# Two attentions on one core: where the local attention's exponentials, the small reciprocals and the reload of old rows stand in the schedule

## The chip, the cores and the metric

The kernel runs on one core of a Trainium2 chip, as one launch. The metric is the device time of an execution in microseconds. Before the change three executions took 1604.45, 1605.76 and 1606.44 us; their median, 1605.76 us, is the time before.

## What is computed

Two attention layers over 2048 positions of width 576, each with 32 heads of 18 columns; their outputs stand side by side in `out` (2048 x 1152, float32).

```
A: qkv = x @ wqkv
   logits[s, w] = q[s] . k[s - 2w] * 18**-0.5     w = 0..7, masked where s - 2w < 0
   o[s] = sum over w of softmax(logits[s])[w] * v[s - 2w]
   out[:, :576] = concat of heads(o) @ wo
B: qkv = x @ wqkv
   o = softmax(q @ k.T * 18**-0.5) @ v            every position against every position
   out[:, 576:] = concat of heads(o) @ wo
```

A is a local attention with a window of eight positions; B is full attention. Products with weights are formed from high and low parts of each operand, so one product is three matmuls.

## The kernel before, in words

**Stages.** Until about 420 us the kernel projects the inputs of A and B to queries, keys and values and stores them in DRAM. Then comes the main loop (L1283), which is the attention of B with everything else woven into it. After it only the last sums are left.

**The main loop.** B's 32 heads are 8 groups of 4 (`g`), its queries 4 blocks of 512 (`b`), its keys 16 tiles of 128 (`kt`): 8 x 4 x 16 = 512 steps, step = 64 g + 16 b + kt. A step computes four score tiles of 128 x 512 (`score`, L262; the matmul is L269), takes the exponential of each on ScalarE (L277) and sums the weighted values of the step before on TensorE (`weigh`, L739; the matmuls are L742). So that the exponentials don't overflow, each query's maximum over its keys is needed before its scores: `maximum` (L224) and `parts_of_maximum` (L239) compute score tiles a second time, some blocks ahead (matmul L158), and VectorE reduces each (L166). A plain step has three of these reductions. When a block's maxima are complete, VectorE folds and transposes them (L176, L183), GpSimd splits them in high and low parts (L101, L102) and `place` (L191, its eight DMAs on L195) puts them into two rows of the block's queries; the block's first score waits for these DMAs.

**Double steps.** A's output projection is 32 sums of 288 columns (`sums_of_a`, L1007). Each is woven into two steps that are issued as one (`together`, L1238): eight scores, eight maxima, the matmuls of the sum (L1256), and on ScalarE the copy of the sum (L1276). `MADE` (L45) has for each of A's eight blocks `j` the four steps in which a sum becomes ready; the double step is the next step and the one after it.

**The agenda.** All other work is planned by hand: `plan(start, pieces)` (L111) puts functions at step numbers, and `due()` (L115) issues those of a step behind the step's own work. An engine executes what it was given in that order, so a piece on VectorE, ScalarE, GpSimd or in SyncE's DMA queue holds up all that was issued behind it on the same engine. After a double step the pieces of its first step are issued, then `weigh`, then those of its second step.

**A's attention** (`local`, L900) for block `j` begins at step `AT[j]` = 10, 67, 123, 178, 233, 288, 343, 398. GpSimd multiplies queries with shifted keys (`match`, from AT + 5), VectorE takes the maximum over the window in three halvings (`most`, L941, AT + 31, 32, 33), GpSimd subtracts it (`lower`, L947, AT + 33), ScalarE takes one exponential of 128 x 512 (`exponents`, L950, AT + 35), VectorE adds over the window in three halvings (`total`, L941, AT + 36, 37, 38) and takes two reciprocals (`inverses`, L957, AT + 38, 39), GpSimd scales (`share`, L960, AT + 39) and weighs the values (`weighted`). All of that from `most` on stands `soon` steps earlier; `soon` (L1022) is 3 for j = 0 and 0 otherwise. The result goes through DRAM (`dao`) and comes back in the layout of the sums by `get` (L984), eight steps ahead of the first of its two sums.

**The end of a block of B** (`finish`, L747): the sums' accumulator `po` is copied out as `o`; its denominators are gathered by a small DMA `den<-o` (L785) one step later, VectorE takes their reciprocals (L786) at 8 steps, they go to DRAM (`drec<-den`, L787, 9 steps) and come back spread over the partitions (`rec<-drec`, L788, 13 steps); GpSimd scales and splits (L789 to L791, from 20 steps) and the result is stored in `do` (L777, 26 steps). In the last group the offsets are 1, 6, 7, 10, 13 to 16 (L784).

**The last group** also computes B's output projection. `fetch_old` (L1047) brings back the rows of the 28 heads before (`old rows`), for each block of queries in four chunks of two DMAs, into room that the keys and queries of group 6 held: those of block 0 are `qs<-do`, those of block 1 `ks<-do`. The weights come as `y<-wob` (`load_wo`, L849). All these DMAs are issued by SyncE, in the order of the agenda, and each waits for the landing of the DMA issued eight before it, because the queue has eight semaphores that are used in turn.

Of the kernel before, what the change touches and what calls it, by code (L numbers as in the profile page):

```python
# [22 lines left out]
NG = H // 4  # L23
# [5 lines left out]
NJ = S // AB  # L29
# [3 lines left out]
STEPS = NB * NT  # L33
# [8 lines left out]

AT = [10, 67] + [13 + 55 * j for j in range(2, S // AB)]

MADE = ((88, 96, 112, 128), (144, 160, 176, 192), (200, 208, 224, 240), (253, 256, 272, 288),  # L45
        (307, 320, 336, 352), (362, 368, 384, 400), (417, 432, 440, 448), (474, 476, 478, 480))


def ap(t, *dims):
# [10 lines left out]
def two_attentions(ctx: ExitStack, tc, xa, wa, woa, xb, wb, wob, out):  # L60
# [50 lines left out]
    def plan(start, pieces):  # L111
        for n, f in pieces:
            agenda[start + n].append(f)
# [267 lines left out]
    with (tc.tile_pool(name="x", bufs=1, side="right") as xp,  # L381
# [103 lines left out]
        if True:  # L485
# [195 lines left out]
            for k in range(2, 14):  # L681
                n = 46 if k == 2 else 36 + 4 * k
# [34 lines left out]
            for c, b in order:  # L717
                n = min(128, 3 * D - 128 * c)
                work_list.append(((b % 2, ws[c][0], xas[b][0], slice(0, n), every),
                                  lambda ps, n=n: ps[:n], lambda ps, c=c, b=b, n=n: leave_a(c, b, n, ps)))  # L720
# [26 lines left out]
    def finish(g, b):  # L747
# [33 lines left out]
                later(2, lambda: stack_new(b))  # L781
                plan(step + 2, full(b))

        times = (1, 8, 9, 13, 20, 21, 22, 26) if g < NG - 1 else (1, 6, 7, 10, 13, 14, 15, 16)  # L784
        for at, f in zip(times, (lambda: load(den, o[DH:128:32]),  # L785
                                 lambda: nc.vector.reciprocal(den, den),  # L786
                                 lambda: load(drec[g, b].rearrange("i (p n) -> (i p) n", n=16), den),  # L787
# [112 lines left out]
    def local(j):  # L900
# [79 lines left out]
        def put(i):  # L980
            load(rows(dao[j, i, 0, 0], (DH * SUB, 128), (1, DH * SUB)),
                 ap(st["parts"][i].bitcast(F32), (1, DH * SUB)))
# [24 lines left out]
        def sums_of_a(h, n, alone=True):  # L1007
# [7 lines left out]
            if not alone:  # L1015
# [3 lines left out]
            behind_scores.append(lambda: nc.vector.tensor_add(y, one, y))  # L1019


        soon = 0 if j else 3  # L1022
        pieces = [(33, lower), (35, exponents), (39, share), (60, upper), (61, rest), (64, lambda: put(0)), (66, lambda: put(1))]

        pieces[:0] = [(at, lambda f=f, n=n: f(n)) for f, ats in ((most, (31, 32, 33)), (total, (36, 37, 38)),
                                                                (inverses, (38, 39))) for n, at in enumerate(ats)]
        for c in range(DH // 2):
            pieces.append((39 + 5 * c // 2, lambda c=c: weighted(c)))
        pieces = [(at - soon, f) for at, f in pieces]
        pieces += [(5 + 5 * c // 2, lambda c=c: match(c)) for c in range(DH // 2)]  # L1030

# [2 lines left out]
        pieces += [(16 + 2 * i, lambda i=i: fetch("v", i)) for i in range(4)]  # L1034
        made = [p - AT[j] for p in MADE[j]]
        for n, ends in enumerate((made[:2], made[2:])):
            pieces.append((ends[0] - 8 if not n else max(ends[0] - 8, made[1] + 1) if j < NJ - 1 else made[0] - 8, lambda n=n: get(n)))
            for h in range(2):
                pieces.append((ends[h], lambda h=h, n=n: finished(h, n)))
                producing.add(AT[j] + ends[h] + 1)  # L1040
            pieces.append((ends[1] + 6, lambda n=n: load(out[p0 + 128 * n : p0 + 128 * n + 128, :D], ys["a", j, n])))
# [50 lines left out]
    sums = {}  # L1092
# [125 lines left out]
    for g in range(1, NG):  # L1218
        if g > EARLY:
            plan(STEPS * (g - 2) + 1, [(n, f) for n, f in enumerate(stack_loads(g))])  # L1220
        if g == NG - 1:
            plan(STEPS * g, [(4, lambda: fetch_old(0)), (10, lambda: fetch_old(1, 0, 2)), (14, lambda: fetch_old(1, 2, 4)),
                             (34, lambda: fetch_old(3)),
                             (38, lambda: fetch_old(2))])
            plan(STEPS * g, [(n, lambda t=t, h=h: partial(t, h)) for n, (t, h) in
                             zip((43, 44, 45, 47, 49, 51), [(t, h) for t in range(3) for h in range(2)])])
            plan(STEPS * g, [(62, lambda: outside.append(lambda: first(3, NB - 1, 0)))])
            for b in range(NB - 1):
                producing.update(STEPS * g + NT * (b + 1) + (23, 15, 7)[b] + n for n in range(8))
        plan(STEPS * (g - 1), [(24, lambda g=g: load_v(g))])  # L1230
# [135 lines left out]
```

## Time and profile before

| | |
|---|---|
| three executions | 1604.45, 1605.76, 1606.44 us |
| the profiled execution | 1607.17 us |
| its span, first to last instruction | 1605.4 us |
| TensorE busy | 1586.9 us |
| VectorE busy | 1363.3 us |
| ScalarE busy | 1214.7 us |
| GpSimd busy | 965.1 us |

The span is one execution on the chip; about 1.8 us of the profiled time lie outside it. The main loop's steps can be found in the trace by the score matmuls on L269: there are 2048 of them, four to a step, so the first of step s is number 4s. Step 449 begins at 1397.4 us, step 464 at 1429.7 us, step 470 at 1442.0 us. A busy engine in the profile is one that has an instruction open; matmuls on different rows of the array overlap, so a busy TensorE isn't one that could do no more.

### The profile page before, as it was taken

Reading aid. Unit: us, or ns where it says so; the run is one execution under the profiler, and the core shown is the slowest. Engines: PE = TensorE matmul, PEld = TensorE weight load, DVE = VectorE, ACT = ScalarE, POOL = GpSimd, SP = SyncE. Lnnn points to the kernel's source line nnn. Section 1 sums busy time; section 2 is a strip of 40 time slices with the busy share of each in tenths; the row PEclk is TensorE's granted clock in tenths of the full one; section 3 lists DMA queues with packets and bytes.
Section 4 is the critical chain, followed back from the end, with each engine's and each line's share of the span. In section 5 each row is a group of like instructions: output and inputs, shape, how many; then the busy total and the mean of one; then the engine's idle time right before and its main releaser. Section 6 shows DMA issues by size and latency. Waiting matters only on the chain.

```text
span 1605.4 us, 34964 instructions
## 1 busy us (share of the span) xinstructions
PE 1586.9 (99%) x13276; PEld 962.1 (60%) x13276; DVE 1363.3 (85%) x2315; ACT 1214.7 (76%) x2438; POOL 965.1 (60%) x798
## 2 busy tenths in 40 slices
PE   9999999999999999999999999999999999998998
PEld 7999888999543445444445445445445445445676
DVE  5199899999999999999999999999999999897622
ACT  6423441221699999999999999999999999996655
POOL 2405742211166995895896896797797799780000
PEclk9999999999999999999999999999999999999999
DMA  8937954532312362255326325422632231153311
GB/s 252 235 127 194 263 167 127 159 101 70 73 41 63 75 144 75 58 120 105 73 75 141 77 86 125 102 81 53 139 102 66 61 97 49 51 178 119 130 61 62
DMA packets 188025, 175.66 MB, mean 109 GB/s; under 512 B 119416, under 2 KB 133240, under 8 KB 186128
## 3 DMA queue, kind: packets, MB, share of 16 engines
q1 hardware_dynamic: 182992, 161.88, 37.2%
q0 software_dynamic: 4032, 10.63, 3.2%
q8 instruction: 104, 1.70, 0.5%
q10 hardware_dynamic: 832, 0.92, 0.2%
q14 instruction: 65, 0.53, 0.1%
HBM read 98.77 MB, written 73.47 MB: 107 GB/s over the span
## 4 chain that ended last, share of the span: by engine, by line
PE 90%; DVE 4%; DMA 2%; ACT 1%; POOL 1%; issue 0%; SPq 0%; POOLq 0%; DVEq 0%
PE po L742 28%; PE bank L269 18%; PE bank L158 17%; PE bank L364 15%; PE bank L301 5%; PE bank L1256 4%; PE bank L1129 4%; DVE mx L166 3%; DMA den<-o 1%; ACT e L277 1%; POOL xlo L412 1%; DMA dqk<-olo 1%; PE bank L516 0%; DMA more<-xa 0%; DVE as L941 0%
## 5 line engine op out<-in xcount | busy, mean ns | idle before, releaser
L166 DVE TENSOR_REDUCE mx<-bank 128x2 f32<-128x512 f32 x2048 | 1278.3, 682 | 129.6 <-PE bank L158 95.9
L277 ACT ACTIVATE e<-bank 128x512 f32<-128x512 f32 x2048 | 1047.1, 607 | 71.9 <-PE bank L269 67.1
L158 PE MATMUL bank<-ks,qs 54*128 54x512 f32 (+1 forms) x2466 | 792.6, 382 | 9.6 <-DVE mx L166 8.1
L158 PEld LDWEIGHTS bank<-ks,qs 54*128 54x128 f32 x2466 | 405.6, 185 | 394.3 <-DVE mx L166 345.3
L269 PE MATMUL bank<-qs,ks 56*128 56x512 f32 x2048 | 598.1, 427 | 0.0
L742 PE MATMUL po<-e,v 128*19 128x512 f32 x4096 | 532.4, 599 | 0.0
L269 PEld LDWEIGHTS bank<-qs,ks 56*128 56x128 f32 x2048 | 310.3, 185 | 31.2 <-ACT e L277 24.6
L923 POOL TENSOR_TENSOR pr<-aq,akv 128x1024 f32<-128x1024 f32 x72 | 158.4, 2201 | 15.8 <-DMA akv<-da 13.0
L966 POOL TENSOR_TENSOR pr<-lg,akv 128x1024 f32<-128x1024 f32 x72 | 158.2, 2197 | 0.6
L742 PEld LDWEIGHTS po<-e,v 128*19 128x19 f32 x4096 | 73.9, 97 | 138.3 <-issue 132.9
L927 POOL TENSOR_TENSOR pr<-pr 128x1024 f32<-128x1024 f32 x64 | 152.5, 2383 | 5.0
L692 ACT ACTIVATE ohi<-bank 128x512 f32<-128x512 f32 (+1 forms) x56 | 30.4, 595 | 150.2 <-issue 115.7
L364 PE MATMUL bank<-xhi,ahi 64*128 64x512 f32 (+1 forms) x448 | 113.7, 388 | 0.0
L364 PE MATMUL bank<-xhi,alo 64*128 64x512 f32 (+1 forms) x448 | 109.7, 388 | 0.0
L364 PE MATMUL bank<-xlo,ahi 64*128 64x512 f32 (+1 forms) x448 | 106.7, 388 | 0.1
L1256 PE MATMUL bank<-wohi,at 64*128 64x288 f32 x480 | 103.4, 305 | 0.0
L967 POOL TENSOR_TENSOR pr<-pr 128x512 f32<-128x512 f32 x72 | 92.5, 1284 | 5.6
L1256 PEld LDWEIGHTS bank<-wohi,at 64*128 64x128 f32 x480 | 74.8, 184 | 27.5 <-ACT e L277 23.8
L412 POOL TENSOR_TENSOR alo<-raw,ahi 128x512 fp32r<-128x512 f32 (+1 forms) x14 | 17.6, 1254 | 121.0 <-ACT ahi L411 121.0
L504 POOL TENSOR_TENSOR olo<-olo,ohi 128x512 fp32r<-128x512 f32 x36 | 46.1, 1294 | 65.6 <-ACT ohi L503 56.4
L101 POOL CAST mh<-mt 128x32 fp32r<-128x32 f32 x32 | 6.7, 210 | 111.5 <-DVE mt L183 111.5
L1256 PE MATMUL bank<-wolo,at 64*128 64x288 f32 x240 | 70.1, 292 | 0.0
(202 smaller groups left out, 1847.8 us busy)
## 6 DMA issues: line engine op xcount, KB each, us to landing
do<-n SPq DMA_DIRECT2D x30, 512.0 KB
da<-ohi SPq DMA_DIRECT2D x52, 256.0 KB
akv<-da SPq DMA_DIRECT2D x64, 175.5 KB
out<-y SPq DMA_DIRECT2D x32, 288.0 KB
qs<-dqk SPq DMA_DIRECT2D x30, 288.0 KB
ks<-dqk SPq DMA_DIRECT2D x30, 288.0 KB
at<-dao SPq DMA_DIRECT2D x60, 128.0 KB
rec<-drec SPq DMA_DIRECT2D x29, 256.0 KB
```

What stands on the lines that cost most here:

```text
L158: return nc.tensor.matmul(ps if part is None else ps[:, 256 * r : 256 * r + 256], qs[at, b, p, 128 * t : 128 * t + 128], ks[at, p, 512 * k ...
L166: nc.vector.tensor_reduce(at, ps.rearrange("q (s n) -> q s n", s=2), axis=AX.X, op=ALU.max)
L269: nc.tensor.matmul(ps, ks[at, p, 128 * kt : 128 * kt + 128], qs[at, b, p], start=True, stop=True)
L277: nc.scalar.activation(e, ps, AF.Exp, scale=SCALE)
L301: nc.tensor.matmul(ps, a, b, start=c == i == 0, stop=c == 4 and i == 1)
L364: nc.tensor.matmul(ps, a, b, start=start, stop=stop)
L742: nc.tensor.matmul(po[32 * i : 32 * i + 19], vs[g][:, kt, 19 * i : 19 * i + 19], es[i], start=kt == 0, stop=kt == NT - 1)
L923: nc.gpsimd.tensor_mul(pr, ap(st["q"][:, 2 * c], (SUB, 2), (0, W), (1, SUB)), window(st["k"], c))
L927: nc.gpsimd.tensor_add(st["pr"], st["pr"], pr)
L966: nc.gpsimd.tensor_mul(at, ap(st["lg"], (0, 2), (SUB, W), (1, SUB)), window(st["v"], c))
L967: nc.gpsimd.tensor_add(at[:, :, :4], at[:, :, :4], at[:, :, 4:])
L1256: return nc.tensor.matmul(ps, a, b, start=r == k == 0, stop=r == 1 and k == len(both[1]) - 1)
```

## The change

Three things move; no instruction is added or removed. (1) `MADE` and a new table `SOON` put A's exponentials of j = 1, 3, 4, 5, 6 into double steps (steps 102, 213, 267, 322, 377): double steps move from 89, 97 to 97, 102, from 201 to 213, from 254 to 267 and from 363 to 377, or the exponential moves one step earlier (j = 4, 5, 6, with `most`, `lower`, `total`, `inverses` and `share`). For j = 1, 3, 4, 6, 7 the second halving of `total` moves up to the step of the first, the third by one step. For j = 2 the `get` of the first pair stands 12 steps ahead instead of 8. (2) In all groups but the last, the denominators' reciprocals go from 8 to 10 steps behind the block's end, the two DMAs behind them from 9 to 11 and from 13 to 14. (3) In the last group the old rows of block 1 are fetched 6 and 12 steps into the group instead of 10 and 14.

```diff
-MADE = ((88, 96, 112, 128), (144, 160, 176, 192), (200, 208, 224, 240), (253, 256, 272, 288),
-        (307, 320, 336, 352), (362, 368, 384, 400), (417, 432, 440, 448), (474, 476, 478, 480))
+MADE = ((96, 101, 112, 128), (144, 160, 176, 192), (208, 212, 224, 240), (256, 266, 272, 288),
+        (307, 320, 336, 352), (368, 376, 384, 400), (417, 432, 440, 448), (474, 476, 478, 480))
+
+SOON = (3, 0, 0, 0, 1, 1, 1, 0)
...
-        times = (1, 8, 9, 13, 20, 21, 22, 26) if g < NG - 1 else (1, 6, 7, 10, 13, 14, 15, 16)
+        times = (1, 10, 11, 14, 20, 21, 22, 26) if g < NG - 1 else (1, 6, 7, 10, 13, 14, 15, 16)
...
-        soon = 0 if j else 3
-        pieces = [(33, lower), (35, exponents), (39, share), (60, upper), (61, rest), (64, lambda: put(0)), (66, lambda: put(1))]
-
-        pieces[:0] = [(at, lambda f=f, n=n: f(n)) for f, ats in ((most, (31, 32, 33)), (total, (36, 37, 38)),
-                                                                (inverses, (38, 39))) for n, at in enumerate(ats)]
+        soon = SOON[j]
+        sums = ((36, 37, 38), (38, 39)) if j in (0, 2, 5) else ((36, 36, 37), (38, 39))
+        late = soon % 3
+        pieces = [(33, lower), (35, exponents), (39, share), (60 + late, upper), (61 + late, rest), (64 + late, lambda: put(0)), (66 + late, lambda: put(1))]
+
+        pieces[:0] = [(at, lambda f=f, n=n: f(n)) for f, ats in ((most, (31, 32, 33)), (total, sums[0]),
+                                                                (inverses, sums[1])) for n, at in enumerate(ats)]
         for c in range(DH // 2):
-            pieces.append((39 + 5 * c // 2, lambda c=c: weighted(c)))
+            pieces.append((39 + 5 * c // 2 + late, lambda c=c: weighted(c)))
...
-            pieces.append((ends[0] - 8 if not n else max(ends[0] - 8, made[1] + 1) if j < NJ - 1 else made[0] - 8, lambda n=n: get(n)))
+            pieces.append((ends[0] - (12 if j == 2 else 8) if not n else max(ends[0] - 8, made[1] + 1) if j < NJ - 1 else made[0] - 8, lambda n=n: get(n)))
...
-            plan(STEPS * g, [(4, lambda: fetch_old(0)), (10, lambda: fetch_old(1, 0, 2)), (14, lambda: fetch_old(1, 2, 4)),
+            plan(STEPS * g, [(4, lambda: fetch_old(0)), (6, lambda: fetch_old(1, 0, 2)), (12, lambda: fetch_old(1, 2, 4)),
```

## The prediction, made before the changed kernel ran

> **What bounds the kernel now.** I read the page first, then the stretches of the main loop by their score matmuls, then the waits, and last the queue of SyncE where a wait led into it.
>
> ```profile
> span 1605.4 us, 34964 instructions
> PE 1586.9 (99%) x13276; PEld 962.1 (60%) x13276; DVE 1363.3 (85%) x2315; ACT 1214.7 (76%) x2438; POOL 965.1 (60%) x798
> ...
> PE 90%; DVE 4%; DMA 2%; ACT 1%; POOL 1%; issue 0%; SPq 0%; POOLq 0%; DVEq 0%
> ```
>
> TensorE carries 90% of the chain that ended last, but VectorE (85%) and ScalarE (76%) are not far behind, so small work on them can come through. The next rows are stretches counted by score matmuls (start:end, length, TensorE busy with the matmul count, weight loads, granted clock, DMA share, GB/s); four matmuls are one step.
>
> ```profile
> 1413.38:1429.65 16.27, 8.90 (x32) 4.74 (x32) 1.00 0.35 116
> 632.79:645.59 12.80, 7.05 (x24) 3.63 (x24) 1.00 0.25 68
> 877.03:890.49 13.46, 7.00 (x24) 3.63 (x24) 1.00 0.71 187
> 994.56:1007.27 12.71, 7.06 (x24) 3.65 (x25) 1.00 0.71 170
> 1119.73:1132.60 12.87, 7.12 (x24) 3.63 (x24) 1.00 0.73 138
> 1240.72:1253.52 12.80, 7.06 (x24) 3.63 (x24) 1.00 0.38 99
> 1366.07:1376.67 10.60, 5.58 (x20) 2.97 (x20) 1.00 0.30 81
> 741.46:748.28 6.82, 3.32 (x12) 1.78 (x12) 1.00 0.62 153
> 1442.00:1457.42 15.42, 5.73 (x16) 3.26 (x16) 0.78 0.58 160
> ```
>
> The first is a quiet stretch: 16.27/8 = 2.03 us a step. The next five are six steps each around A's exponentials of j = 1, 3, 4, 5, 6; six quiet steps would be 12.20, so they are 0.60, 1.26, 0.51, 0.67 and 0.60 too long, 3.6 us together. The seventh, five steps behind j = 7, is 0.43 too long. The eighth, three steps from 152 on, is 0.7 too long, and the last, steps 470 to 473, is 15.42 - 8.14 = 7.3 too long. These 12 us are all that the change can win.
>
> **The exponentials.** A plain step has no room on ScalarE:
>
> ```profile
> 879.49 0.65 ACT L950 ACTIVATE lg<-lg 128x512 f32<-128x512 f32 x1
> 880.01 7.81 ACT L277 ACTIVATE e<-bank 128x512 f32<-128x512 f32 x15
> ...
> 1365.49 0.69 ACT L950 ACTIVATE lg<-lg 128x512 f32<-128x512 f32 x1
> 1366.68 2.06 ACT L277 ACTIVATE e<-bank 128x512 f32<-128x512 f32 x4 [0.50 <-PE bank L269]
> ```
> ```profile
> 1366.21 0.43 DVE L941 TENSOR_TENSOR as<-lg 128x256 f32<-128x256 f32 x1 [0.76 <-ACT lg L950]
> 1368.72 0.28 DVE L941 TENSOR_TENSOR as<-as 128x128 f32<-128x128 f32 x1
> ```
>
> Behind A's exponential of j = 3 (879.49) fifteen of B's follow without a pause: it takes 0.52 us (879.49 to 880.01) of an engine with none to spare. For j = 7, which stands in a double step already, ScalarE idles 0.50 us afterwards for TensorE. So j = 7 shows what the change makes of five others, and in the changed program's order on ScalarE the exponentials of j = 1, 3 to 7 do stand behind the copy of a sum. VectorE's first sum then waits 0.76 us, which costs nothing as long as the double step has left VectorE ahead. Moving the second sum to that place brings 0.28 us more there and takes it from a plain step.
>
> What stays of the excess in each stretch lies between 0 and the 0.43 of j = 7, whose five steps hold a fold of maxima too; I take 0.25, so 5 x 0.25 = 1.25 stay and **2.4 us go** (1.5 to 3.6). The number of double steps is the same, so what one costs drops out.
>
> ```profile
> 1109.38 1.29 POOL L930 TENSOR_TENSOR lg<-pr 128x512 f32<-128x512 f32 x1
> ```
> ```profile
> 1111.97 0.42 DVE L941 TENSOR_TENSOR am<-lg 128x256 f32<-128x256 f32 x1
> ```
> ```profile
> 1451.13 1.15 SPq L996 DMA_DIRECT2D aq<-dao  x2
> 1454.82 0.54 SPq L787 DMA_DIRECT2D drec<-den  x1
> 1456.64 0.58 SPq L788 DMA_DIRECT2D rec<-drec  x1
> ```
>
> Two costs I put at nothing. `most` of j = 4, 5, 6 needs GpSimd's last product. At j = 5 that ends at 1110.67, and `most`, 1111.97 before, would come a step earlier, at 1109.94: VectorE would wait 0.7 us. But GpSimd's work since the `share` of j = 4 moves with it by that step, so between 0 and 0.7 I take 0. And for j = 3 `get` of the second pair now waits for the double step at 267 and must land by 273: four plain steps and a bit more, some 9 us. Its six copies take 0.6 us each to issue (1451.13), 3.5 together, and then between the 1.8 us of a small copy in a free queue (1454.82 to 1456.64) and the 10.7 us of one in a full queue (below). Near 5 it is covered; at 10.7 it costs some 5 us.
>
> **The small reciprocals.**
>
> ```profile
> DVE den L786 <- DMA den<-o: 0.8, 1, 0.8
> ```
>
> Up to 1440 us there is one such wait, at step 153, where the eighth stretch lost 0.7. Two steps more are 4 us, so it goes. The reciprocal now meets the first `most` at step 154 and the sums of j = 6 at 378, some 0.1 each. **0.5 us go** (0.2 to 0.7). The two DMAs behind it have GpSimd's multiplication, still 20 steps behind the block's end, as their cover: six steps, 12 us; a late one delays only GpSimd, which waits for VectorE later in each block of A anyhow.
>
> **The last group.** The long stretch at step 470:
>
> ```profile
> 1438.99 10.70 DMA den<-o
> ```
> ```profile
> 1449.78 0.25 DVE L786 RECIPROCAL den<-den 128x16 f32<-128x16 f32 x1 [5.24 <-DMA den<-o]
> ```
> ```profile
> 1445.00:1451.00 6.00, 1.15 (x10) 0.14 (x8) 1.22 (x3) 1.62 (x4) 0.00 (x0) 0.86 0.41 112
> 1451.00:1455.00 4.00, 3.77 (x18) 1.65 (x18) 2.65 (x5) 2.06 (x4) 0.00 (x0) 0.50 0.71 161
> ```
>
> The denominators' 8 KB take 10.7 us to land, because they stand at the end of a full queue; VectorE waits 5.24 us and all behind it with it. The granted clock (the column behind the five engines) then falls to 0.50, which is the rest: 7.3 - 5.24 = 2.0 us. The queue:
>
> ```profile
> 1401.63 6.64 SPq L1066 DMA_DIRECT2D qs<-do  x8
> 1408.95 1.48 SPq L856 DMA_DIRECT2D y<-wob  x2
> 1419.51 2.31 SPq L195 DMA_DIRECT2D qs<-mh  x4
> 1421.93 2.16 SPq L195 DMA_DIRECT2D qs<-mt  x4
> 1424.13 3.18 SPq L1066 DMA_DIRECT2D ks<-do  x4
> ```
> ```profile
> 1401.60:1420.60 19.00, 19.00 (x156) 8.00 (x152) 16.87 (x30) 17.95 (x37) 18.15 (x18) 1.00 0.49 157
> 1420.60:1424.60 4.00, 4.00 (x33) 1.67 (x32) 3.70 (x7) 4.00 (x9) 3.77 (x4) 1.00 0.04 8
> 1424.60:1449.70 25.10, 21.55 (x168) 8.58 (x166) 18.39 (x30) 21.95 (x44) 15.18 (x14) 0.99 0.61 196
> ```
> ```profile
> ks<-do SPq DMA_DIRECT2D x8, 252.0 KB
> ```
> ```profile
> 1429.66 0.49 PE L269 MATMUL bank<-qs,ks 56*128 56x512 f32 x1
> ```
>
> From 1420.6 to 1424.6 the DMAs stand still (8 GB/s): SyncE was at `place` (L195), and the old rows behind it came only then. The change puts four of the eight `ks<-do` ahead of `place`, behind `out<-y`. Four are 1008 KB, 1.03 MB: 5.3 us at the second stretch's 196 GB/s, 6.6 at the first's 157. I take 6.2 off the second stretch, nearer to the rate at which such loads made up most of the traffic. Against that, the first stretch ends between those two later; I take the middle, 5.9, so at 1426.5, and since an issue waits for the landing eight before it, `place`'s last copy waits for the second `y<-wob`, then: it is issued at 1426.7 instead of 1423.6, and all behind it about 2.9 us later. Net the denominators land 3.3 us earlier, at 1446.4. The wait left is 5.24 - 3.3 = 1.9 us. Ends: the loads fill only the hole and none of the second stretch gets shorter by more than the delay (nothing won), or the wait goes altogether.
>
> The clock: at a floor of 0.50, a mean of 0.86 over 6 us means 1.7 us low, so it fell near 1449.3, some 4 us after TensorE began to starve; a wait of 1.9 ends before, and the 2.0 us go. Together **5.3 us go** (0 to 7.3).
>
> The Trainium skill, "TensorE: Matmul & The Clock Gate", Part 1, says that the array falls to half its clock after an idle window of about 3.4 us, and that the window runs free, so the moment varies. By it a remaining wait of 1.9 us costs no clock, but one near 3 might; the fall to 0.50 in the row above agrees. With the clock lost all the same, the sum would be 2.0 us worse.
>
> The one thing this could break: the queries' maxima that `place` brings are for the block that starts at step 464, whose first score ran at 1429.66. In the changed kernel the last should be issued at 1426.7 and, at the small copy's 1.8 us, land at 1428.5, 1.2 us ahead. Behind step 471 I see nothing that takes the gain back: the DMAs that the next double steps wait for stand behind the same queue and come earlier with it, and the later ones are issued when the engines get there.
>
> **The sum.** 2.4 + 0.5 + 5.3 = 8.2 us. The profiled execution took 1607.17 us, 1.8 outside its span; it would take 1599.0, its span 1597.2. The runs' median is 1.4 lower than the profiled execution: 1605.76 - 8.2 = **1597.6 us**.
>
> **The rivals.**
> *The hole only moves.* The four loads delay `place` and what follows by as much as they free, and the denominators land as late as before. For: the first stretch ran at 157 GB/s, at which the loads take 6.6 us. Against: the hole was 4 us long and the loads can fill it. Time: 1605.76 - 2.9 = 1602.9; with half the gain 1600.2.
> *The exponentials' stall changes its engine.* VectorE is 85% busy; with three small operations and a 0.76 us wait behind a double step it could lose what ScalarE wins, as j = 7 still loses 0.43. Then only the reciprocals and the last group count: 1605.76 - 5.8 = 1600.0.
> *Slower: `place` comes too late.* The old rows stand ahead of it, TensorE stops at step 464, and past some 4 us the clock falls as well. From a lateness of about 8 us: 8 + 2.0, then a new wait for the denominators of about 3, against 2.9 won and the 7.3 of the old stall: about 1609. For that 1.03 MB would have to take 15 us, 68 GB/s; the two stretches above ran at 157 and 196.
> *It doesn't do what it says.* The order on ScalarE and in SyncE's queue shows that it does.
>
> **How the numbers follow.** Forecast 0.70 (its own range 1594.5 to 1600.0); the hole only moves 0.14, half of it above 1602.5; the stall changes its engine 0.10; slower 0.05; more than forecast 0.01. A measurement can tell about 0.2% from no change, 3.2 us: the border is at 1602.5. Faster 0.70 + 0.07 + 0.10 + 0.01 = 0.88, same 0.07, slower 0.05. The range goes from 1594.3, where the whole wait and 3.6 us of the exponentials go, to 1602.0: left out are 0.05, 0.08 and some 0.05 within the forecast's tails.
>
> **What would show it.** In the profile after: the wait `DVE den L786 <- DMA den<-o` down from 5.24 to under 2.5 us, and no clock of 0.50 near step 471; TensorE not waiting at step 464; the five stretches of six steps at 12.2 to 12.6 us; no wait on `den` at step 153. Wrong would be a wait of TensorE for `qs` at step 464, for `at` at step 273, or new excess of half a us in the steps behind the moved double steps.

## The result, and the profile after

| | before | after |
|---|---|---|
| median of 11 executions | 1605.35 us (1604.00 to 1608.57) | 1601.34 us (1596.93 to 1603.45) |
| ratio | | 0.9971, 95% interval 0.9961 to 0.9980 |
| profiled execution, its span | 1607.17, 1605.4 us | 1600.95, 1599.2 us |
| start of step 1, in the profile | 420.50 us | 419.10 us |
| from the start of step 1 to the end | 1184.86 us | 1180.06 us |

By the medians the change makes the kernel 4.0 us faster; the ratio puts it at 4.7 us (3.2 to 6.3). The forecast was 8.2 us; the time lies in the range (1594.3 to 1602.0), near its upper end. Of the 6.2 us between the two spans, 1.4 stand ahead of step 1, in the projections, which the change doesn't touch (in the profile of before the granted clock stood at 0.50 for 3.41 us there, from 176.1 us on; in that of after it didn't). Over all fourteen profiles of this study the start of step 1 lay between 418.15 and 421.35 us, so below the traces are compared from there on: 4.8 us, of which 2.3 lie in steps 1 to 470 and 2.5 behind.

The first lines of the page after:

```profile
span 1599.2 us, 34971 instructions
PE 1583.9 (99%) x13276; PEld 966.4 (60%) x13276; DVE 1365.8 (85%) x2315; ACT 1214.7 (76%) x2438; POOL 965.4 (60%) x798
...
PE 90%; DVE 4%; DMA 3%; ACT 2%; POOL 1%; issue 0%; POOLq 0%; DVEq 0%; SPq 0%
```

Nothing shows there: the same work, and the same shares within 1%. The stretches by steps do show it. The next rows are windows of the changed kernel (start:end, length, then TensorE, its weight loads, VectorE, ScalarE, GpSimd, granted clock, DMA share, GB/s):

```profile
635.46:647.77 12.31, 12.31 (x100) 5.22 (x97) 12.02 (x26) 11.64 (x24) 5.00 (x4) 1.00 0.59 158
878.55:890.81 12.26, 12.26 (x100) 5.22 (x97) 12.08 (x24) 11.63 (x24) 7.26 (x8) 1.00 0.67 181
997.88:1006.50 8.62, 8.62 (x71) 3.83 (x69) 8.34 (x19) 7.90 (x16) 1.43 (x2) 1.00 0.60 132
1116.15:1128.60 12.45, 12.34 (x100) 5.23 (x97) 11.64 (x23) 11.74 (x25) 3.12 (x3) 1.00 0.74 137
1239.26:1251.98 12.72, 12.72 (x103) 5.52 (x101) 12.31 (x24) 12.02 (x24) 5.41 (x4) 1.00 0.48 132
1362.26:1372.69 10.43, 10.33 (x86) 4.27 (x82) 10.13 (x22) 9.84 (x21) 3.05 (x2) 1.00 0.30 81
739.53:745.66 6.13, 6.13 (x53) 2.62 (x50) 5.70 (x10) 6.13 (x14) 4.06 (x6) 1.00 0.68 153
980.54:989.78 9.24, 8.21 (x70) 3.47 (x66) 8.95 (x15) 8.16 (x18) 5.46 (x5) 1.00 0.67 168
1438.32:1451.17 12.85, 9.69 (x70) 3.99 (x66) 7.60 (x14) 8.23 (x18) 4.69 (x5) 0.87 0.58 148
```

The first six are the plain steps behind the double step that now has the exponential of j = 1, 3, 4, 5, 6, 7 (six steps; four for j = 4; five for j = 7). A quiet step is 2.03 us, and the step right ahead of a double step is 0.33 longer in both kernels (the third and the fifth row end with one). What is left over is 0.11, 0.06, 0.15, 0.25, 0.19 and 0.26, together 1.0, where it was 4.1: **3.1 us went**. The seventh row, steps 152 to 154, lost its 0.7. The last, steps 470 to 473, is 12.85 us where it was 15.42: 2.6 went, 4.7 are left.

The eighth row is new: steps 262 to 265 took 9.24 us, 1.1 more than four quiet steps, and the excess is in step 264 alone. In the kernel before, this step has none. Its rows, VectorE's and GpSimd's:

```profile
985.04 1.46 DVE L943 TENSOR_TENSOR am<-lg 128x256 f32<-128x256 f32 x1
```
```profile
984.93 1.29 POOL L793 TENSOR_TENSOR n<-o,n 128x512 fp32r<-128x512 f32 x1
```

In the kernel before, where it stood a step later, this maximum took 0.41 us:

```profile
992.80 0.41 DVE L941 TENSOR_TENSOR am<-lg 128x256 f32<-128x256 f32 x1
```

Now it stands beside a GpSimd operation that began 0.11 us ahead of it, and it ends 0.28 us behind that one's end. There was no wait in VectorE's row, no idle gap and no releaser: the 1.0 us is inside the instruction.

The remaining stall of the last group:

```profile
1432.38 11.69 DMA den<-o
```
```profile
1444.16 0.25 DVE L788 RECIPROCAL den<-den 128x16 f32<-128x16 f32 x1 [3.31 <-DMA den<-o]
```
```profile
1445.61 0.38 PE L160 MATMUL bank<-ks,qs 54*128 54x256 f32 x1 [3.16 <-DVE mx L168]
```
```profile
1445.00:1447.00 2.00, 1.39 (x12) 0.88 (x16) 1.89 (x4) 0.85 (x2) 1.10 (x1) 0.80 0.71 161
1447.00:1449.00 2.00, 2.00 (x11) 0.32 (x12) 1.14 (x2) 1.21 (x3) 0.00 (x0) 0.50 0.72 163
1449.00:1451.00 2.00, 2.00 (x16) 1.06 (x16) 1.19 (x2) 1.37 (x3) 0.00 (x0) 0.85 0.70 173
```

Counted from the start of step 449 (1393.72 us, 1397.44 before), the denominators' 8 KB were issued 2.9 us earlier than before, and they were 11.7 us on the way instead of 10.7: 1.9 us won. VectorE still waited 3.31 us, TensorE stood 3.16 us, and the clock still fell to 0.50 after it. The forecast was a wait of 1.9 us and no fall.

### The profile page after: what moved, and what is told of

Read it like the earlier page. It is cut to its first block, busy times and chain, and to the rows that moved or that the text cites. A ratio compares the mean times of both kernels' runs of the same rounds, so it can differ in the third digit from the quotient of the medians.

```text
span 1599.2 us, 34971 instructions
## 1 busy us (share of the span) xinstructions
PE 1583.9 (99%) x13276; PEld 966.4 (60%) x13276; DVE 1365.8 (85%) x2315; ACT 1214.7 (76%) x2438; POOL 965.4 (60%) x798
## 4 chain that ended last, share of the span: by engine, by line
PE 90%; DVE 4%; DMA 3%; ACT 2%; POOL 1%; issue 0%; POOLq 0%; DVEq 0%; SPq 0%
PE po L744 29%; PE bank L271 18%; PE bank L160 17%; PE bank L366 14%; PE bank L303 5%; PE bank L1133 4%; PE bank L1260 4%; DVE mx L168 3%; DMA dqk<-olo 1%; DMA den<-o 1%; ACT e L279 1%; POOL xlo L414 1%; DMA dqk<-ohi 1%; DMA first<-wb 0%; DVE am L943 0%
## 5 line engine op out<-in xcount | busy, mean ns | idle before, releaser
L366 PEld LDWEIGHTS bank<-xhi,ahi 64*128 64x128 f32 (+1 forms) x448 | 65.0, 181 | 2.7
```

Source lines behind the costliest of these rows:

```text
L366: nc.tensor.matmul(ps, a, b, start=start, stop=stop)
```

## The experiments

The theory after the result: the three parts act in their own places and add up; two things were mis-sized. First, the maximum of j = 4 now meets a GpSimd operation (1.1 us). Second, the denominators came 1.9 us earlier against the steps instead of 3.3, because 1.03 MB of old rows still stand ahead of them in SyncE's queue, and this leaves a wait that is still long enough for the clock. Rivals: step 264 was an accident of one execution; the DMA engines are full whatever the order of the queue.

### Each part alone

Part 1 alone is the changed kernel with the two other edits taken back; parts 2 and 3 are the kernel before with one edit each:

```diff
 part 1 (to the changed kernel):
-(1, 10, 11, 14, 20, 21, 22, 26)
+(1, 8, 9, 13, 20, 21, 22, 26)
-(6, lambda: fetch_old(1, 0, 2)), (12, lambda: fetch_old(1, 2, 4)),
+(10, lambda: fetch_old(1, 0, 2)), (14, lambda: fetch_old(1, 2, 4)),
 part 2 (to the kernel before):
-(1, 8, 9, 13, 20, 21, 22, 26)
+(1, 10, 11, 14, 20, 21, 22, 26)
 part 3 (to the kernel before):
-(10, lambda: fetch_old(1, 0, 2)), (14, lambda: fetch_old(1, 2, 4)),
+(6, lambda: fetch_old(1, 0, 2)), (12, lambda: fetch_old(1, 2, 4)),
```

> The kernel before with part 1 alone: the tables of double steps and exponentials, with nothing moved in the small reciprocals and in the last group. Theory (each part acts in its own steps, and their sum is the whole): the stretches of j = 1, 3, 4, 5, 6, 7 give back 3.3 us and step 264 costs 1.1 us, so -2.2 us against the kernel before (1603.1), and step 264 is 1.1 us too long again because VectorE's first maximum over the window of j = 4 takes some 1.4 us beside a GpSimd operation instead of 0.4. Rival (the stall at step 264 was one execution's accident): step 264 has no excess and the kernel wins 3.3 us (1602.0). The wait at step 153 stays at 0.7 us and the stretch from step 470 stays 7.3 us too long by both.

> The kernel before with part 2 alone, the small reciprocals two steps on. One look, since 0.7 us is less than the times can tell: step 153 loses its 0.7 us of excess, the waits for the small gather up to 1440 us are gone, and steps 154 to 156 and 376 to 380 get no more than 0.2 us longer. Rival (the wait only moves): the same 0.5 to 0.7 us stand at step 155 or at GpSimd's multiplication ten steps later.

> The kernel before with part 3 alone, the old rows of block 1 fetched 6 and 12 steps into the last group. Theory (a queue in order: the gather lands when what stands ahead of it has landed, about 1.9 us earlier against the steps than before): -2.6 us (1602.7), the wait for the denominators about 3.3 us, the granted clock still falling behind it. Rival (what the prediction had: 3.3 us earlier): a wait of 1.9 us, full clock, -5.3 us (1600.0). Rival (the hole only moves): no change.

| | median | ratio to before | steps 1 to 470 | step 264 | steps 471 to 473, excess |
|---|---|---|---|---|---|
| before | 1605.40 us | | | 0.0 | 7.3 us |
| part 1 | 1602.53 us | 0.9980 (0.9971 to 0.9989) | -1.8 us | 0.3 us | 7.0 us |
| part 2 | 1605.55 us (one run) | | -1.3 us | 0.0 | 7.3 us |
| part 3 | 1602.61 us | 0.9980 (0.9971 to 0.9990) | 0.0 us | 0.0 | 4.3 us |

Part 3 did by itself what it does in the changed kernel: a wait of 2.90 us, and the clock fell all the same. Part 2 took the 0.7 us at step 153 and left no wait for the small gather ahead of step 470; another 0.5 us went at step 217, where VectorE's last halving of j = 3 took 0.21 us instead of 0.62 (the meetings with GpSimd, below). That isn't the work of part 2: part 3 alone, whose instructions there are those of the kernel before, has 0.21 us for that halving too, and its steps 215 to 217 are 0.6 us shorter than in the profile of before. The three runs don't simply add up to the change: from step 1 on they won 2.2, 1.4 and 2.9 us, 6.6 together, against its 4.8 (the largest differences: 0.8 at step 264, 0.7 in steps 200 to 223, 0.7 in steps 471 to 473). Part 1 is not quite either theory: step 264 was 0.3 us too long, not 1.1 and not 0. Its rows say why:

```profile
985.33 0.64 DVE L943 TENSOR_TENSOR am<-lg 128x256 f32<-128x256 f32 x1
```
```profile
983.74 1.28 POOL L791 TENSOR_TENSOR o<-o,rec 128x512 f32<-128x512 f32 x1
985.09 0.61 POOL L792 CAST n<-o 128x512 fp32r<-128x512 f32 x1
985.78 1.33 POOL L793 TENSOR_TENSOR n<-o,n 128x512 fp32r<-128x512 f32 x1
```

GpSimd's three operations stood 0.6 us later against the step than in the changed kernel. The maximum met the rest of the second one (until 985.70) and was done 0.2 us into the third; it took 0.22 us more than its 0.42. The price of the meeting is what is left of the GpSimd operation that is open when VectorE's begins. Over the fourteen profiles, 171 of A's maxima and sums of 128 x 256 began with no GpSimd operation open, and took 0.41 to 0.43 us; three began beside one that only fills a tile, and took no longer; 50 began beside one that reads a tile, and each ended 0.28 us or more behind that one's end. Two more such meetings, of 1.54 us at step 215 and of 0.96 at step 374, made these steps of part 1 longer than in the changed kernel by 0.8 and 0.5 us.

### Step 264: move the maximum away

The first trial moves the exponential with it, the second only the maxima and the subtraction:

```diff
 the exponential too (to the changed kernel):
-SOON = (3, 0, 0, 0, 1, 1, 1, 0)
+SOON = (3, 0, 0, 0, 0, 1, 1, 0)
 the maxima alone (to the changed kernel):
-(33, lower)
+(34 if j == 4 else 33, lower)
-(most, (31, 32, 33))
+(most, (32, 33, 34) if j == 4 else (31, 32, 33))
```

> The changed kernel with the exponential of j = 4 a step later (its entry in the table of early steps is 0): most at 264, 265, 266 issues one step later than in the changed kernel, and the exponential stands at the second step of the same double step. Theory (VectorE's first maximum is held up by GpSimd's subtraction of high parts, which began 0.1 us before it, and the meeting goes when the maximum comes a step later): that maximum takes 0.42 us again instead of 1.46, step 264 has no excess, 1.1 us less than the changed kernel (1600.2). Rival (it is the place in step 264 or 265, right ahead of the double step, and not the meeting): the excess moves to step 265 and nothing is won (1601.3).

> The changed kernel with only the maxima over the window of j = 4 and GpSimd's subtraction behind them one step later; the exponential and everything behind it stay where the change put them. Theory (the stall of step 264 is the meeting of VectorE's 128 x 256 maximum with GpSimd's subtraction of high parts, and the exponential has a step to spare): the maximum takes 0.42 us, step 264 has no excess, steps 270 and 319 stay as in the changed kernel: 1.1 us less (1600.2). Rival (the exponential then waits for GpSimd): ScalarE's exponential starts later than in the changed kernel and the double step or step 270 gives back 0.5 us or more.

The maxima alone: 1599.73 us median, ratio 0.9964 (0.9951 to 0.9976). VectorE, GpSimd and steps 262 to 265:

```profile
988.51 0.42 DVE L943 TENSOR_TENSOR am<-lg 128x256 f32<-128x256 f32 x1
```
```profile
986.37 1.28 POOL L793 TENSOR_TENSOR n<-o,n 128x512 fp32r<-128x512 f32 x1
```
```profile
981.99:990.18 8.19, 8.19 (x68) 3.46 (x65) 7.77 (x14) 8.19 (x18) 5.45 (x5) 1.00 0.69 169
```

The maximum is 0.42 us again and the four steps take 8.19 us instead of 9.24; steps 270 and 319 are as in the changed kernel. The theory holds. With the exponential moved too (1600.35 us, ratio 0.9966, 0.9954 to 0.9979), step 264 lost its 1.1 us as well, but 0.5 us came at step 270 and 1.0 at step 319:

```profile
1106.70 0.43 DVE L943 TENSOR_TENSOR am<-lg 128x256 f32<-128x256 f32 x1 [0.94 <-POOL lg L932]
```

That is the wait that the prediction named for j = 5 and put at 0 because GpSimd's work "moves with it by that step". Here j = 4's share didn't move, and the wait is there, 0.94 us. So that argument was right.

Both trials also had 0.6 to 0.8 us at step 215, which the changed kernel's profile doesn't have, though all three have the same instructions up to there. VectorE and GpSimd at that place, in the trial with the exponential moved:

```profile
877.25 0.43 DVE L943 TENSOR_TENSOR as<-lg 128x256 f32<-128x256 f32 x1 [0.29 <-ACT lg L952]
877.71 1.30 DVE L943 TENSOR_TENSOR as<-as 128x128 f32<-128x128 f32 x1
```
```profile
877.57 1.29 POOL L791 TENSOR_TENSOR o<-o,rec 128x512 f32<-128x512 f32 x1 [5.88 <-DMA rec<-drec]
```

The second halving of the sum, 0.29 us by itself, took 1.30 beside a product that GpSimd began when its DMA landed. In the ten profiles with the same instructions up to there, step 215 lost between 0 and 0.8 us. It is the landing of a DMA, some tenths of a us earlier or later, that decides.

### The queue: what stands ahead of the denominators

```diff
 the second half late (to the changed kernel):
-(12, lambda: fetch_old(1, 2, 4)),
+(27, lambda: fetch_old(1, 2, 4)),
 all of it early:
-(6, lambda: fetch_old(1, 0, 2)), (12, lambda: fetch_old(1, 2, 4)),
+(6, lambda: fetch_old(1)),
 one load late, in fetch_old:
-load(o[i].bitcast(F32)[:n], rows(first, (32 * S, 7), (S, DH), (1, 512)))
+f = lambda t=o[i], first=first: load(t.bitcast(F32)[:n], rows(first, (32 * S, 7), (S, DH), (1, 512)))
+later(15, f) if (b, c, i) == (1, 3, 1) else f()
```

> The changed kernel with the second half of block 1's old rows not 12 but 27 steps into the last group, behind the reload of the small reciprocals; the first half stays at 6. Theory (the denominators land late because 1.03 MB of these rows stand ahead of them in one queue): they land about 5.5 us earlier, VectorE doesn't wait for them at step 471, the granted clock stays full, the 4.7 us of excess in steps 471 to 473 go and nothing comes back later: about 1596.6. Rival (the queue ahead is only part of it, and the two 590 KB writes of the changed kernel's local attention and the reload of 262 KB that stand there hold it up all the same): a wait of 1 to 2 us stays, 1598 to 1599. Rival (the rows come late for the place where they go): a new wait near steps 476 to 494 gives the gain back (1601).

> The changed kernel with all four chunks of block 1's old rows 6 steps into the last group, ahead of the maxima's small copies. This tries the prediction's slower case, that the small copies come too late for step 464, by 1 MB more ahead of them. With two chunks ahead the last small copy landed 0.3 us before the first score of step 464. Theory (the queue runs at some 180 GB/s and in order): 1.03 MB are 5.7 us more, the first score of step 464 waits for about 5.4 us, and as no old rows are left behind the copies the denominators land with no wait at step 471; in sum about 2 us slower than the changed kernel (1603). Rival (the small copies pass the large loads, since each is only 2 KB on a few of the 16 DMA engines): no wait at step 464 and no wait at step 471, about 4.7 us faster (1596.6).

> The changed kernel with one of the eight loads of block 1's old rows, the last, moved 15 steps back, behind the denominators (258 KB less ahead of them). One look. Theory (order within the queue; a load of this size took 1.4 us there): the denominators land about 1.4 us earlier and VectorE waits about 1.9 us for them, which is the wait that the prediction forecast. What it said of the clock is then tried by itself: with the clock at full speed throughout, the excess of steps 471 to 473 is about 1.9 us (2.8 us less than the changed kernel's 4.7). Rival (the clock falls after a shorter gap in TensorE's work too): the granted clock falls behind the wait and the excess is 3 us or more.

With the second half late (1598.06 us, ratio 0.9949, 0.9937 to 0.9961) there is no wait for the denominators and no fall of the clock; the 4.7 us are gone. Nothing came back at the place where the rows are used. But the time is 1.5 us above the forecast of 1596.6, and the trace has 0.4 of it at step 464, which began late (and 0.2 at step 509); another 1.2 stand ahead of step 1, where in this profile, too, the clock was at 0.50 for 3.41 us.

```profile
1427.47 0.46 PE L271 MATMUL bank<-qs,ks 56*128 56x512 f32 x1 [0.42 <-ACT e L279]
```

The last small copy of `place` landed at 1427.17, by the semaphore's count in the trace. The row names ScalarE, but it is the first score of the block, which reads what the copy brings. The first half of the old rows alone can put `place` at the edge.

With all of it early (1602.35 us, one run), the slower case of the prediction came true in its mechanism. The first score of step 464 waited:

```profile
1430.73 0.76 PE L271 MATMUL bank<-qs,ks 56*128 56x512 f32 x1 [4.69 <-DMA y<-wob]
```

The row names a load of weights (with which the copies share their semaphores in turn); the last copy landed at 1430.49. Steps 463 and 464 were 6.3 us too long, 1.4 of it behind the wait, with the clock at 0.50 for 3.41 us, and steps 471 to 473 had no excess. Against the changed kernel this is 6.1 lost and 4.7 won.

With one load late (1598.83 us, one run), the wait was 1.35 us instead of the 1.9 of its theory, TensorE's gap 1.19, the excess 1.23, and the clock stayed at 1.00. All profiles with a wait for the denominators at step 471 (the last columns are the excess of steps 471 to 473, the least work that TensorE had there in one of the clock's cells of 3.41 us, which the text below explains, and the lowest clock of a 2 us window there):

| kernel | VectorE's wait | TensorE's gap | excess | least work in a cell | lowest clock |
|---|---|---|---|---|---|
| before | 5.24 us | 5.08 us | 7.29 us | 0.26 us | 0.50 |
| part 1 alone | 5.09 us | 4.93 us | 7.02 us | 0.65 us | 0.50 |
| part 2 alone | 4.96 us | 4.81 us | 7.26 us | 0.00 us | 0.50 |
| after | 3.31 us | 3.16 us | 4.71 us | 0.59 us | 0.50 |
| part 3 alone | 2.90 us | 2.76 us | 4.30 us | 1.72 us | 0.50 |
| maxima of j = 4 later | 2.13 us | 1.98 us | 2.05 us | 2.15 us | 1.00 |
| exponential of j = 4 later | 1.89 us | 1.73 us | 1.79 us | 2.04 us | 1.00 |
| one load late | 1.35 us | 1.19 us | 1.23 us | 2.22 us | 1.00 |

```profile
1447.18 0.38 PE L158 MATMUL bank<-ks,qs 54*128 54x256 f32 x1 [2.76 <-DVE mx L166]
```
```profile
1445.48:1448.90 3.42, 1.72 (x16) 0.85 (x16) 3.05 (x6) 1.18 (x3) 0.67 (x1) 1.00 0.67 151
1448.90:1452.31 3.41, 3.41 (x20) 1.51 (x16) 2.64 (x5) 2.92 (x6) 0.00 (x0) 0.50 0.75 170
```
```profile
1444.86 0.38 PE L160 MATMUL bank<-ks,qs 54*128 54x256 f32 x1 [1.98 <-DVE mx L168]
```
```profile
1440.73:1444.15 3.42, 2.15 (x20) 0.88 (x16) 1.29 (x4) 2.64 (x6) 2.23 (x3) 1.00 0.23 63
1444.15:1447.56 3.41, 2.70 (x22) 1.46 (x24) 3.16 (x7) 2.16 (x5) 0.94 (x1) 1.00 0.74 169
```

The first three lines are part 3 alone, the others the maxima of j = 4 later. Where the clock falls, the excess is 1.4 us more than the wait (1.9 to 2.3 with the waits of about 5 us); where it stays, the excess is some 0.1 us less than the wait. But it isn't the length of the gap that decides. In each of the fourteen profiles all changes of the granted clock lie whole multiples of 3.41 us apart, and it stays low for one or more cells of this length. Cut into these cells, the profiles between 10 and 1580 us show a border: from full speed the clock fell behind each cell in which TensorE was busy for 1.72 us or less (eleven cells), and behind none in which it was busy for 1.76 us or more. So what counts is how much of a gap lies in one cell. In the run with the second half late, a gap of 1.82 us in the projections lay in one cell and lost the clock:

```profile
175.18 0.50 PE L366 MATMUL bank<-xhi,whi 64*128 64x512 f32 x2 [1.82 <-ACT olo L504]
```
```profile
172.17:175.59 3.42, 1.60 (x15) 1.12 (x13) 1.76 (x3) 2.66 (x5) 2.00 (x3) 1.00 1.06 352
175.59:179.00 3.41, 3.41 (x20) 2.66 (x18) 1.71 (x3) 3.30 (x7) 3.33 (x3) 0.50 0.97 299
```

The gap of 1.98 us with the maxima of j = 4 later lay across two cells and lost nothing. Where the cells lie against the steps differs from profile to profile: the one in which step 471 begins had its start 0.97 us ahead of that step in the changed kernel, 0.04 us ahead with the maxima later. No run sets where the cells lie, so this is read from the fourteen profiles and not tried by itself, and the ends of matmuls are modelled, so the border is as good as that model.

The two trials on j = 4 have the changed kernel's last group, instruction for instruction. Their denominators landed 3.1 and 3.4 us earlier against the steps than before, which is the prediction's 3.3, and the excess is near the prediction's 1.9. In the profile of the changed kernel it was 1.9 us earlier, in part 3 alone 2.0. The rate of the loads goes with it: from the issue of the first `qs<-do` to the landing of the second `y<-wob`, 3.97 MB, SyncE's queue moved 152 GB/s in the changed kernel and 154 in part 3 alone, 160 and 163 in the trials with the maxima and with the exponential later; over the ten profiles with these loads in this order it was 149 to 164. SyncE's rows for the small copies, which wait for those loads, show it; the changed kernel first, then the maxima of j = 4 later:

```profile
1415.48 4.60 SPq L197 DMA_DIRECT2D qs<-mh  x4
1421.06 3.57 SPq L197 DMA_DIRECT2D qs<-mt  x4
```
```profile
1416.03 3.21 SPq L197 DMA_DIRECT2D qs<-mh  x4
1420.24 3.48 SPq L197 DMA_DIRECT2D qs<-mt  x4
```

Why the loads are slower in some executions than in others, the traces don't show.

### Another queue

```diff
 (to the changed kernel; or nc.gpsimd)
-lambda: load(den, o[DH:128:32])
+lambda: (nc.scalar.dma_start if g == NG - 1 else load)(den, o[DH:128:32])
```

> The changed kernel with one DMA on another queue: the gather of the denominators in the last group is issued by ScalarE instead of SyncE. The old rows and all else stay where they are. Theory (order within one queue): in a queue of its own the 8 KB pass the loads that are under way and land 2 to 5 us after the issue, by 1437 us, so VectorE doesn't wait at step 471, and the 4.7 us of steps 471 to 473 go, less some tenths for ScalarE's issue (about 1596.8). Rival (the sixteen DMA engines are full with the 3.3 MB that were issued before, and a queue of its own doesn't help): the gather lands near 1444 us as it does now, and the time stays at 1601.

> The changed kernel with the gather of the last group's first denominators issued by GpSimd instead of SyncE; ScalarE's queue held ScalarE for 17.3 us. One look. Theory (order within one queue): in a queue of its own the 8 KB pass the loads under way, land within 2 to 5 us of their issue, and VectorE doesn't wait at step 471; the excess of steps 471 to 473 goes, 4.7 us less than the changed kernel (1596.6). Rival (the DMA engines are full, whatever the queue): it lands near 1444 us and the excess stays. A third case is that GpSimd is held as ScalarE was; then its row shows the wait, and the question stays open.

From ScalarE (1617.57 us, one run) it failed as an experiment: the issue held ScalarE.

```profile
ACT e L279 <- DMA den<-o: 17.3, 1, 17.3
```
```profile
1448.87 1.15 ACTq L787 DMA_DIRECT2D den<-o  x1
```

The issue came 0.2 us after a DMA of SyncE had landed (1448.71) that counts on the same semaphore in the trace. That the two engines share the semaphores that are used in turn is the likely reason; it wasn't tried apart. From GpSimd, whose DMA counts on a semaphore that SyncE doesn't use, the question was settled (1596.10 us, one run):

```profile
1430.63 0.73 POOL L787 DMA_DIRECT2D den<-o  x1
```
```profile
DMA to landing us min/median/max: 5.7/5.7/5.7
```
```profile
1440.45 0.24 DVE L788 RECIPROCAL den<-den 128x16 f32<-128x16 f32 x1
```

With the old rows and all else in place, the same 8 KB took 5.7 us instead of 11.7 (12.2 and 12.4 in the two trials on j = 4), the reciprocal had no wait, and the excess of steps 471 to 473 was 0. The DMA engines were no less busy: their share was 0.82 over these 5.7 us, and 0.65 over the 11.7 of the changed kernel. It is the place in the queue that costs. The loads of this run moved 164 GB/s, so its gain is to be set against the excess of the trials on j = 4, 1.8 and 2.1 us, rather than against the 4.7.

### Both together

> The changed kernel with both edits: the exponential of j = 4 a step later, and the second half of block 1's old rows 27 steps into the last group. Theory (the two costs stand in different steps and add): 1.1 + 4.7 = 5.8 us less than the changed kernel, about 1595.5; ratio to the kernel before about 0.9938. Rival (something else, such as TensorE's own work, sets the end once these are gone): less than 4 us won, over 1597.3.

> The same edit together with the second half of block 1's old rows 27 steps into the last group. Theory: both gains add, without the 0.5 and 1.0 us at steps 270 and 319 that the later exponential of j = 4 brought. Against the run in which the rows alone are late (1598.06) it is 1.1 us less, about 1597.0, ratio to the kernel before about 0.994. Rival (phases shift and VectorE meets GpSimd elsewhere): the same 1598, with an excess of a similar size at another step between 200 and 460.

| | median | ratio to before | from step 1 to the end |
|---|---|---|---|
| the change | 1601.34 us | 0.9971 (0.9961 to 0.9980) | 1180.06 us |
| exponential of j = 4 later, rows late | 1597.54 us | 0.9947 (0.9935 to 0.9959) | 1176.81 us |
| maxima of j = 4 later, rows late | 1596.27 us | 0.9943 (0.9931 to 0.9956) | 1174.97 us |

Both are faster than both kernels, and the intervals of their ratios lie below that of the change. The first lost 1.5 us at steps 270 and 319 again and had 1597.5 us, where its theory said 1595.5. That is beyond the 1597.3 at which its rival began, but the loss stands in these two steps and not, as the rival had it, in TensorE's own work. The second is the best of the study. Its steps 262 to 265 and 470 to 473:

```profile
980.30:988.49 8.19, 8.19 (x69) 3.47 (x65) 7.77 (x14) 8.19 (x18) 5.51 (x5) 1.00 0.69 168
1436.91:1445.05 8.14, 8.14 (x70) 3.49 (x66) 7.71 (x14) 8.14 (x18) 1.26 (x1) 1.00 0.67 176
```

Both are quiet now: 8.19 and 8.14 us, at full clock. 0.8 us were left at step 215.

## Why the prediction was right, and where it was not

**Direction and place: right.** All three parts won where the prediction said, and in the main by the mechanism that it gave: ScalarE's exponential fits into a double step, the wait at step 153 goes with two steps more, and the old rows fill the hole at `place`. **The size: about half.** 1601.34 us lies outside the range that the forecast had for itself (1594.5 to 1600.0), between the times that the prediction gave its rival "The hole only moves" (1600.2 with half the gain, 1602.9). It lies in the range only because that was stretched to 1602.0. Two of the prediction's own signs failed: the wait of under 2.5 us and the clock without 0.50 near step 471.

**The exponentials: 3.1 us instead of 2.4,** within the 1.5 to 3.6. About 1.0 stays instead of 1.25. Some 0.6 of the 3.1 is luck: of the 1.26 us that the prediction read at j = 3 as ScalarE's, a part was two halvings on VectorE that met GpSimd in that profile (0.83 and 0.62 us). In part 3 alone, with the same instructions there, they took 0.28 and 0.21.

**"Two costs I put at nothing": the step that failed first.** The two named there cost nothing: no wait of TensorE at step 273, no wait of `most` for GpSimd in the changed kernel. But j = 4's `most`, one step earlier, meets GpSimd's subtraction of a block of B, and this 1.1 us was in no term. The prediction counted for each engine what it waits for, and not what runs beside it on another engine. An excess of half a us or more was its own sign of being wrong, though it looked for it behind the moved double steps and not ahead of them. The Trainium skill, "SBUF — State Buffer", section "Who interferes with whom", has the rule: a VectorE instruction with two inputs in SBUF contends with a GpSimd instruction that reads SBUF, and the one that is issued second blocks until the first is done. This case agrees: 1.46 us against 0.42 where GpSimd began 0.11 us earlier, 0.42 again when it was moved away.

**The small reciprocals: right,** 0.73 us at step 153 against 0.5. What the prediction said of late DMAs behind it ("a late one delays only GpSimd, which waits for VectorE later") is not the whole: when GpSimd starts late it meets A's sums, as step 215 shows.

**The last group: 2.6 us instead of 5.3, the larger miss.** Two steps failed. The first is the size in "Net the denominators land 3.3 us earlier". In the profiled execution it was 1.9 and in part 3 alone 2.0, with the loads ahead at 152 and 154 GB/s; the two trials on j = 4 had 3.1 and 3.4. (By the prediction's own times the delay behind `place` is 1426.7 - 1423.6 = 3.1 us and not 2.9; measured against the steps, the last copy was issued 4.3 us later in the changed kernel, 2.9 and 2.4 in the trials with the maxima and with the exponential later.) The second is "some 4 us after TensorE began to starve; a wait of 1.9 ends before". The clock doesn't go by the time since TensorE began to starve, but by the work in a cell of 3.41 us. With waits of 1.89 and 2.13 us the two trials kept the clock, as forecast, but their gaps lay across two cells, which is luck: 1.82 us in one cell lost it elsewhere. The wait that came in the changed kernel left 0.59 us of work in one cell, and brought 1.4 us of clock with it. The prediction said that with a wait "near 3" the clock might fall, and gave this no chance of its own. The times of the changed kernel lie at 1600.7 to 1603.5 in nine of eleven runs and at 1596.9 and 1599.5 in two. That fits with the clock lost in most executions, and so does the mean granted clock of each run (0.999 in those two, 0.997 or 0.998 in eight of the nine), but only one of them has a trace.

On the clock, the Trainium skill, "TensorE: Matmul & The Clock Gate", Part 1, speaks of an idle window of about 3.4 us that runs free. The traces agree with the window's length, 3.41 us, and with its place against the steps differing from run to run. They differ on the idleness, and the measurement decides: a window with 1.72 us of work in it lost the clock, one with 1.76 us didn't.

**The rivals.** "The hole only moves" is refuted for the whole (the wait fell by 1.9 to 3.4 us in the four profiles with these loads and the gather on SyncE's queue). "The exponentials' stall changes its engine" is refuted for five of six; for j = 4 something like it happened, by another mechanism. "Slower: `place` comes too late" was real with 1.03 MB more ahead of it: a wait of 4.7 us and 1.4 behind it, where the prediction had 8 and 2. In the changed kernel the last copy landed 0.3 us ahead of the first score instead of the 1.2 forecast. The score that did wait for it, in the run with the second half late, began 0.3 us behind the landing as well, so in the changed kernel's profile nothing was left of the margin; with the maxima of j = 4 later the copy landed 1.65 us ahead.

**The sum.** Forecast -8.2. From step 1 on, the profile gives 3.1 for the exponentials, 0.7 for the reciprocals, 2.6 for the last group, less 1.1 at step 264 and 0.5 in small excesses of 0.1 to 0.3 us in about ten steps whose cause stays open: 4.8. The medians say 4.0.

## What to carry to other kernels

When an operation moves, look at what the other engines have open at its new place, not only at what it waits for: the loss stands inside an instruction's duration, so compare the mean of a group with its longest, and look for a short two-input operation that ended just behind its neighbour on GpSimd.

A small transfer that somebody waits for is as late as everything ahead of it in its queue. Put the bulk that is needed later behind it, or give it another queue, before trying to make the bulk faster.

Where TensorE is to stand for about two us or more, the forecast isn't one number but two: here 1.82 us in one of the clock's cells lost the clock, and 1.98 us across two cells didn't. Which one comes may differ from run to run: give each a chance.

## What the runs showed of the hardware that was not expected

- VectorE's maximum of 128 x 256 from two SBUF operands took 0.42 us alone, 1.46 us beside a GpSimd subtraction that began 0.11 us earlier, and 0.64 us when it met the last 0.37 us of a GpSimd copy. The halving of 128 x 128 took 0.29 and 1.30 us. In all 50 cases in which a 128 x 256 operation began beside a GpSimd operation that reads a tile, it ended 0.28 us or more behind that one's end.
- TensorE's clock changed only on a grid of 3.41 us. From full speed it fell to 0.50 behind each of these cells with 1.72 us of TensorE's work or less, and behind none with 1.76 or more. So a gap of 1.82 us lost it and one of 1.98 us didn't.
- 8 KB took 11.7 us at the end of SyncE's queue and 5.7 us in GpSimd's, with the same loads under way.
- A DMA that ScalarE was to issue held ScalarE's own work for 17.3 us.
